# Gated linear attention with a feed-forward layer: longer runs in the first loads, another form of the weight conversion, other places for its steps

## The chip, the cores and the metric

The kernel runs on one core of a Trainium2 chip. The metric is the device time of one execution in microseconds. The engines named here are TensorE (PE, with PEld for its weight loads), VectorE (DVE), ScalarE (ACT), GpSimd (POOL) and SyncE (SP). SP issues every DMA of this kernel, in one queue.

## What is computed

There are 4 batches of 8 heads, 768 tokens and 48 numbers a head, and then a feed-forward layer over all 3,072 tokens. The inputs `q`, `k`, `v` and `alpha` are float32; both weight matrices come as float64.

```python
for t in range(S):
    state = alpha[:, :, t, :, None] * state + np.einsum('bhd,bhe->bhde', k[:, :, t], v[:, :, t])
    y[:, :, t] = np.einsum('bhd,bhde->bhe', q[:, :, t], state)
...
x = np.ascontiguousarray(attn_out.transpose(0, 2, 1, 3)).reshape(B * S, H * D)
...
h = x @ w_in            # 384 to 2048
g = np.maximum(0.01 * h, h)
return (g @ w_out).astype(np.float32)   # 2048 to 384
```

## The kernel before

**Attention.** The work is cut into 24 units: 128 tokens of one batch with all 8 heads. For a unit u, `scans` builds running products of alpha along the tokens (L309) and the products of alpha to the next mark (L315), `scaled_q` and `scaled_k` multiply q and k by them, `scores` multiplies k by q (L351), `mask_scores` copies the scores out on ACT and masks them on POOL, `k_tokens` turns k back, `outputs` adds the masked scores times v to q times the state and splits the result into a high and a low part (L419, L420), and `next_state` updates the state. The units are staggered: scans of unit u+1 are emitted ahead of the scores of unit u.

**Two ways to bring a tile in.** alpha, q and k come with tokens in rows and are needed with the 48 numbers of two heads in rows. For the first nine units (`AHEAD`), `load` (L128) fetches a tile with one token per partition, 8 runs of 48 numbers (192 bytes) each, and `transposed` turns it on PE with four transposes against `ident` (L272) into a PSUM bank. Later units are loaded in runs of four tokens and turned on DVE (L284); this stays. There are two load buffers for each of alpha, q and k (`NL`), so unit u+2 is loaded when unit u has been turned. Each PSUM tile of the attention takes the next of six banks (`bank`, tags "a" and "b" in turn).

**Keeping PE's clock.** `keep_warm` issues fp32 matmuls of `seed` into an idle bank at the start and between the transposes of unit 0. `keep_warm_wide` does so with a tile `zeros` between the transposes of k of unit 0.

**Feed-forward.** Three units (384 tokens) form a block i, eight blocks in all, and the 2,048 inner numbers are cut into 16 slices f. An item is (i, f). `ffn_in` multiplies x by w_in with nine matmuls of 384 columns (high times high, low times high, high times low, over three groups of rows, L487) into one of two banks `ph`, scales on ACT (L490), takes the maximum on DVE (L493), which frees the bank, rounds to the high part on ACT (L495) and takes the low part on DVE (L499). `ffn_out` (L512) multiplies by w_out three items later (`LAG`). Blocks 0 and 1 go first, in turn: (0,0), (1,0), (0,1), (1,1), and so on. Items (0,0) and (1,0) are started beside the last attention units (`STARTS`). Blocks 2 to 7 follow one by one, with the attention of units 9 to 23 woven in between.

**Converting the weights.** [...] Its eight steps before: ACT scales the top words (L238), DVE shifts them (L240) and puts in the sign (L243), ACT rounds to the high part (L246), DVE takes the exponent (L250), subtracts the high part (L252), multiplies the low words by the exponent (L254) and adds both into the low part (L257). `load_weights` fetches slice f into one of four raw buffers with five DMAs. Slices 0 and 1 are converted whole beside units 7 and 8. Slice 2 is converted whole when unit 8 is done, and one step of slice 3 is taken. Later slices are converted in steps between the DVE and ACT instructions of the items of blocks 0 and 1.

**What sets the order.** The framework plans the order on each engine at build time, by its own estimate of durations. Where the code says `tc.issue_after`, or `put(ordered, ...)`, the order is written by hand: every DVE and ACT instruction of items and conversions from (0,1) to the end of block 1 stands in one line per engine. Engines take their instructions in that order; PE, DVE, ACT, POOL and SP meet by semaphores.

Of the kernel before, what the change touches and what calls it, by code (L numbers as in the profile page):

```python
# [9 lines left out]
F32 = mybir.dt.float32  # L10
# [12 lines left out]
def gated_linear_attn_ffn(ctx, tc, q, k, v, alpha, w_in, w_out, out):  # L23
# [29 lines left out]
    NV = 3  # L53
# [5 lines left out]
    LAG = 3  # L59
    SOON, EARLY = 2, 2  # L60
    LEAD = 8
# [11 lines left out]
    def pieces(name, dtype, *shapes):  # L73
# [11 lines left out]

    ident, mask, ones, acc, seed, *rest = pieces(
        "small", F32, (P,), (C,), (1,), (2 * NU,), (NP, C), *[(NP * D,)] * B, *[(DM,)] * NV, *[(NP * PITCH,)] * sum(NL)
    )
# [27 lines left out]
    def load(u, i):  # L116
# [8 lines left out]
        if u < AHEAD:  # L125
            n = H if u or i else H // 2
            for h in range(0, H, n):
                nc.sync.dma_start(  # L128
                    by_token(t)[:, h:h + n, 0:D], src[b, h:h + n, ts, :].rearrange("h t d -> t h d")
                )  # L130
            return
# [21 lines left out]
    nc.vector.memset(ones, 1.0)  # L153
    zeros = cst.tile([P, 4 * C], F32R, name="zeros")
    nc.gpsimd.memset(zeros.bitcast(F32), 0.0)

# [6 lines left out]

    def keep_warm_wide(n):

        for _ in range(2):
            nc.tensor.matmul(idle[:, 0:n], zeros[:, 0:P], zeros[:, 0:n], start=True, stop=True)

    keep_warm(6)
    for i in (0, 1, 2):  # L170
        for t in loads_sb[i]:
            nc.vector.memset(by_token(t)[:, :, D:], 1.0)
    for n in range(max(NL)):
# [3 lines left out]
        load_values(n)  # L177
    make_identity(nc, ident)
    nc.gpsimd.memset(mask, 1.0)
    nc.gpsimd.affine_select(  # L180
# [3 lines left out]
    for i in (0, 1, 2):  # L184
        for t in loads_sb[i]:
            nc.gpsimd.memset(t[:, H * HB:], 1.0)

# [31 lines left out]
    def converting(f, ordered=False):  # L219
# [17 lines left out]
        with nullcontext() if lines["ACT"] else behind("hi", f - 1):  # L237
            put(ordered, "ACT", lambda: nc.scalar.mul(top.bitcast(F32), top.bitcast(F32), 2.0 ** -112))  # L238
        yield
        put(ordered, "DVE", lambda: nc.vector.tensor_scalar(  # L240
            bits, top, 3, 0x7FFFFFF8, ALU.logical_shift_left, ALU.bitwise_and))
        yield
        put(ordered, "DVE", lambda: nc.vector.scalar_tensor_tensor(  # L243
            bits, top, -0x80000000, bits, ALU.bitwise_and, ALU.bitwise_or))
        yield
        made["hi", f] = put(ordered, "ACT", lambda: nc.scalar.copy(hi, val))  # L246
        yield
        pw = cvp.tile([P, 2 * DM], I32, name="pw", bufs=NPW)
        rest = pw.bitcast(F32)
        put(ordered, "DVE", lambda: nc.vector.tensor_scalar(pw, bits, -0x800000, None, ALU.bitwise_and))  # L250
        yield
        put(ordered, "DVE", lambda: nc.vector.tensor_tensor(val, val, hi.bitcast(F32), ALU.subtract))  # L252
        yield
        put(ordered, "DVE", lambda: nc.vector.scalar_tensor_tensor(  # L254
            rest, low.bitcast(U32), 2.0 ** -52, rest, ALU.mult, ALU.mult))
        yield
        made["w", f] = put(ordered, "DVE", lambda: nc.vector.tensor_tensor(lo, rest, val, ALU.add))  # L257

# [7 lines left out]
    def transposed(u, i, name, **kw):  # L266

        src = loaded(u, i)
        if u < AHEAD:
            ps = banks4()  # L270
            for p in range(NP):
                last = nc.tensor.transpose(  # L272
                    ps[:, p, :], by_token(src)[:, 2 * p:2 * p + 2, :].rearrange("t h d -> t (h d)"), ident
                )
                if u == 0 and p % 2:
                    with tc.issue_after(last.ins):
                        if i == 2:
                            keep_warm_wide(4 * C if p == 1 else 2 * C)
                        else:
                            keep_warm(2)  # L280
            return ps
# [196 lines left out]
    def ffn_in(i, f, steps=None):  # L478
# [16 lines left out]
        put(ordered, "ACT", lambda: nc.scalar.copy(gh, t))  # L495
        for step in second:
            next(step, None)
        gl = ffp.tile([P, TB], F32R, name="gl", bufs=LAG + 1)
        made["gl", i, f] = put(ordered, "DVE", lambda: nc.vector.tensor_tensor(gl, t, gh.bitcast(F32), ALU.subtract))  # L499
        return gh, gl  # L500

# [55 lines left out]
    kinds[:] = "a"  # L557

    with behind("x", AHEAD - 1):
        for _ in converting(EARLY, True):  # L560
            pass

    due, emitted, held = 0.0, 0, 0
    new, coming = None, converting(EARLY + 1, True)
    next(coming)
    for n in range(len(items) + LAG):
        slices = 0
        if n < len(items):
# [15 lines left out]
            if n < len(STARTS):  # L584
                pass
            elif i == 0:
                old, new, coming = new or iter(()), coming, converting(f + SOON + 1, True)
                gs[n] = ffn_in(i, f, ((), (coming, new, old, new)))
            elif i == 1:
                gs[n] = ffn_in(i, f, ((new, new), (new,)))  # L590
                next(new, None)
            else:
                gs[n] = ffn_in(i, f)
# [142 lines left out]
```

## Time and profile before

| | |
|---|---|
| Time, median of 3 runs | 538.94 us (538.92 to 539.31) |
| The profiled execution | 538.77 us, its span 537.1 us, granted clock 0.991 |
| PE busy | 518.8 us (97%) in 3,934 instructions |
| DVE busy | 375.0 us (70%) in 703 instructions |
| ACT busy | 234.0 us (44%) in 514 instructions |
| POOL busy | 49.1 us (9%) in 116 instructions |
| DMA | 92,985 packets, 46.67 MB, 57,856 of the packets under 512 bytes |

The span is the time from the first to the last instruction of the profiled execution; the 538.77 us hold what lies around it too. Busy times overlap between engines and say nothing of order. The stages are: units 0 to 8 of the attention and the first conversions up to about 70 us; blocks 0 and 1 of the feed-forward with all other conversions up to about 165 us; blocks 2 to 7 with the other units up to 531 us; and 6 us in which the last results are written.

### The profile page before, as it was taken

The page shows a single profiled execution, that of the slowest core. Times are in us where ns is not written, and L with a number is a line of the kernel's source. Part 1 is how long each engine was busy: PE and PEld are TensorE (multiplying, and loading weights), DVE is VectorE, ACT ScalarE, POOL GpSimd, SP SyncE. Part 2 cuts the span into 40 slices and gives each one's busy share as a digit, 9 for nine tenths or more (in the row PEclk, how much of TensorE's full clock was granted, in tenths as well). Part 3 has the DMA queues.
Part 4 walks back from the last instruction along what each step waited for, and adds up shares of the span by engine and source line. Part 5 has one row for each costly group of instructions (what it writes and reads, how often), then busy time and mean ns, then how long its engine had stood idle before and what let it go on. Part 6 is the DMA issues. An engine that isn't in the chain of part 4 may idle for free.

```text
span 537.1 us, 10383 instructions
## 1 busy us (share of the span) xinstructions
PE 518.8 (97%) x3934; PEld 492.6 (92%) x3934; DVE 375.0 (70%) x703; ACT 234.0 (44%) x514; POOL 49.1 (9%) x116
## 2 busy tenths in 40 slices
PE   8879899999999999999999999999999999999995
PEld 7668789999999899999999999999999999999995
DVE  6778999999988897875675685775777534332331
ACT  2665755555533453435334443344343354233331
POOL 3333510000000011010000001000000000000000
PEclk9999899999999999999999999999999999999998
DMA  9999854454823643533323422523201010001001
GB/s 149 163 179 183 198 140 119 117 131 136 183 53 87 190 117 78 107 81 98 70 67 70 108 69 64 98 50 92 71 0 38 11 35 1 22 1 45 1 1 49
DMA packets 92985, 46.67 MB, mean 87 GB/s; under 512 B 57856, under 2 KB 90112, under 8 KB 92928
## 3 DMA queue, kind: packets, MB, share of 16 engines
q1 hardware_dynamic: 92928, 45.93, 39.0%
q8 instruction: 33, 0.54, 0.4%
q14 instruction: 24, 0.20, 0.1%
HBM read 38.83 MB, written 4.72 MB: 81 GB/s over the span
## 4 chain that ended last, share of the span: by engine, by line
PE 86%; DVE 4%; DMA 3%; issue 2%; ACT 1%; SPq 1%; POOL 1%; ACTq 0%; DVEq 0%; POOLq 0%
PE ph L487 36%; PE b L512 32%; PE a L390 5%; PE a L351 4%; PE a L512 4%; DMA small<-in_alpha_dram 2%; DMA raw<-in_moe_w_in_dram 1%; PE a L374 1%; PE b L272 1%; PE a L411 1%; PE b L390 1%; DVE pc L309 1%; PE b L411 1%; POOL sm L362 1%; DVE rc L315 0%
## 5 line engine op out<-in xcount | busy, mean ns | idle before, releaser
L487 PE MATMUL ph<-large,w 128*128 128x384 f32 x1152 | 227.4, 340 | 2.8 <-DVE t L493 2.8
L487 PEld LDWEIGHTS ph<-large,w 128*128 128x128 f32 x1152 | 201.9, 189 | 5.5 <-DVE t L493 3.9
L512 PE MATMUL b<-w,gh 128*128 128x384 f32 x672 | 170.0, 340 | 0.0
L493 DVE TENSOR_TENSOR t<-ph,t 128x384 f32<-128x384 f32 x128 | 70.5, 551 | 88.7 <-ACT t L490 88.4
L512 PEld LDWEIGHTS b<-w,gh 128*128 128x128 f32 x672 | 119.7, 188 | 2.2 <-issue 0.5
L490 ACT ACTIVATE t<-ph 128x384 f32<-128x384 f32 x128 | 62.6, 489 | 130.1 <-PE ph L487 122.8
L495 ACT CAST gh<-t 128x384 fp32r<-128x384 f32 x128 | 65.7, 514 | 112.8 <-DVE t L493 102.6
L512 PE MATMUL b<-w,gl 128*128 128x384 f32 x336 | 107.4, 336 | 0.0
L499 DVE TENSOR_TENSOR gl<-t,gh 128x384 fp32r<-128x384 f32 x128 | 70.8, 553 | 34.4 <-ACT gh L495 33.2
L512 PEld LDWEIGHTS b<-w,gl 128*128 128x128 f32 x336 | 62.5, 188 | 0.1
L362 POOL TENSOR_SCALAR_AFFINE_SELECT sm<-sm 128x512 f32<-128x512 f32 x33 | 22.8, 705 | 113.3 <-ACT sm L361 113.3
L351 PE MATMUL a<-qs,ks 48*128 48x128 f32 x312 | 30.9, 287 | 0.1
L351 PEld LDWEIGHTS a<-qs,ks 48*128 48x128 f32 x312 | 25.9, 189 | 5.4 <-issue 4.4
L284 DVE STREAM_TRANSPOSE ks<-small 128x512 f32<-128x512 f32 x15 | 16.6, 1121 | 12.3 <-PE a L374 12.3
L390 PE MATMUL a<-sm,small 128*48 128x128 f32 (+1 forms) x312 | 23.2, 282 | 0.1
L319 POOL COPY pe<-pc 128x4 f32<-128x4 f32 x24 | 4.8, 202 | 188.6 <-DVE pc L309 188.6
L309 DVE TENSOR_TENSOR_SCAN pc<-e,small 128x128 f32<-128x128 f32 x60 | 20.1, 398 | 0.5 <-ACT pc L327 0.5
L367 POOL TENSOR_TENSOR small<-us,pe 112x192 f32<-112x192 f32 x20 | 11.9, 594 | 90.2 <-DVE us L432 87.5
L390 PEld LDWEIGHTS a<-sm,small 128*48 128x48 f32 (+1 forms) x312 | 17.1, 132 | 3.2 <-issue 3.0
L361 ACT COPY sm<-a 128x512 f32<-128x512 f32 x24 | 14.0, 585 | 13.8 <-PE b L351 11.1
L512 PE MATMUL a<-w,gh 128*128 128x384 f32 x96 | 20.0, 336 | 0.0
L315 DVE TENSOR_TENSOR_SCAN rc<-e,small 128x511 f32<-128x511 f32 x15 | 19.0, 1270 | 0.2
(86 smaller groups left out, 525.4 us busy)
## 6 DMA issues: line engine op xcount, KB each, us to landing
raw<-in_moe_w_out_dram SPq DMA_DIRECT2D x16, 384.0 KB, 3.9
small<-in_v_dram SPq DMA_DIRECT2D x24, 192.0 KB, 4.0
raw<-in_moe_w_in_dram SPq DMA_DIRECT2D x32, 144.0 KB, 3.9
out_dram<-t SPq DMA_DIRECT2D x24, 192.0 KB, 1.9
small<-in_alpha_dram SPq DMA_DIRECT2D x32, 96.0 KB, 2.3
small<-in_q_dram SPq DMA_DIRECT2D x30, 96.0 KB, 2.2
small<-in_k_dram SPq DMA_DIRECT2D x30, 96.0 KB, 2.2
small<-in_alpha_dram SPq DMA_DIRECT2D x30, 80.0 KB, 2.3
```

Of the source, the lines that this page charges most:

```text
L284: nc.vector.transpose(t.rearrange("r p (j t) -> r p t j", t=T4), src.rearrange("r p (t d) -> r p t d", t=T4)[:, :, :, 0:32],)
L309: nc.vector.tensor_tensor_scan(pc[:, p, :], aT[:, p, :], ones.broadcast_to([P, C]), 1.0, ALU.mult, ALU.mult)
L315: nc.vector.tensor_tensor_scan(flat[2][:, NP * C - 2::-1], flat[0][:, NP * C - 1:0:-1], flat[1][:, NP * C - 2::-1], last, ALU.mult, ALU.add)
L351: nc.tensor.matmul(ss[s][:, p, :], ks[lo:lo + D, p, :], qs[lo:lo + D, p, :], start=True, stop=True)
L362: nc.gpsimd.affine_select(out=sm[s], in_=sm[s], compare_op=ALU.is_ge, fill=0.0, base=0, pattern=[[0, NP], [1, C]], channel_multiplier=-1)
L390: nc.tensor.matmul(y[s][HB * c:HB * c + lhsT.shape[-1], p % 2, :], lhsT, rhs, skip_group_check=True, **kw)
L487: nc.tensor.matmul(ph, w_in_of(f, wn, g), xt[:, g, :], start=n == 0, stop=n == 3 * NG - 1)
L490: put(ordered, "ACT", lambda: nc.scalar.mul(t, ph, 0.01))
L493: put(ordered, "DVE", lambda: nc.vector.tensor_tensor(t, ph, t, ALU.max))
L495: put(ordered, "ACT", lambda: nc.scalar.copy(gh, t))
L499: made["gl", i, f] = put(ordered, "DVE", lambda: nc.vector.tensor_tensor(gl, t, gh.bitcast(F32), ALU.subtract))
L512: nc.tensor.matmul(po[j], gt[:, js], w_out_of(f, wn), start=f == 0 and n == 0, stop=f == NF - 1 and n == 2)
```

## The change

- `load` for the first nine units: partition (j, p) now holds four tokens (4j to 4j+3) of the heads 2p and 2p+1, in two runs of 192 numbers (768 bytes). It is one DMA a tile for unit 0 too, where alpha came in two.
- `transposed` for these units: for each of the four tokens n and each of the two heads s, one ordinary matmul with 64 columns of the tile (48 numbers of the token, then 16 of what follows) as the stationary operand and `turn` as the moving one. `turn` is the identity with its columns reordered; POOL copies it from `ident` once. Each matmul writes 64 partitions and every fourth of 512 columns.
- The memsets at the start follow the new layout; `zeros` and `keep_warm_wide` are gone, and `keep_warm(2)` stands in their place.
- `converting`: the low part no longer comes from the subtraction of the high part. The bits below the high part are cut out of the top word by two shifts in place, added to the scaled low word, and multiplied by the exponent. It is still eight steps, six of them on DVE.
- Places: five of the eight steps of slice 2 stand ahead of the items, the other three in item (0,1). Slice f+1 is finished in item (0,f), and slice f+2 is begun there and carried five steps far by item (1,f). In items with such steps, the low part `gl` (L499) now comes after one step, and the rest of the steps after it.

```diff
-        if u < AHEAD:
-            n = H if u or i else H // 2
-            for h in range(0, H, n):
-                nc.sync.dma_start(
-                    by_token(t)[:, h:h + n, 0:D], src[b, h:h + n, ts, :].rearrange("h t d -> t h d")
-                )
+            nc.sync.dma_start(
+                t[:, 0:2 * PITCH].rearrange("r (s n) -> r s n", s=2)[:, :, 0:RUN],
+                src[b, :, ts, :].rearrange("(p s) (j t) d -> j p s (t d)", s=2, t=T4),
+            )
...
-    zeros = cst.tile([P, 4 * C], F32R, name="zeros")
-    nc.gpsimd.memset(zeros.bitcast(F32), 0.0)
...
+    nc.gpsimd.tensor_copy(turn.rearrange("r (p j) -> r p j", p=NP), ident.rearrange("r (j p) -> r p j", p=NP))
...
         put(ordered, "DVE", lambda: nc.vector.tensor_scalar(
-            bits, top, 3, 0x7FFFFFF8, ALU.logical_shift_left, ALU.bitwise_and))
+            bits, top, 3, 4, ALU.logical_shift_left, ALU.bitwise_or))
...
+        put(ordered, "DVE", lambda: nc.vector.tensor_scalar(
+            top, top, 23, 23, ALU.logical_shift_left, ALU.arith_shift_right))
+        yield
+        pw = cvp.tile([P, 2 * DM], I32, name="pw", bufs=NPW)
+        put(ordered, "DVE", lambda: nc.vector.tensor_scalar(pw, bits, -0x800000, None, ALU.bitwise_and))
+        yield
         made["hi", f] = put(ordered, "ACT", lambda: nc.scalar.copy(hi, val))
         yield
...
-        put(ordered, "DVE", lambda: nc.vector.tensor_tensor(val, val, hi.bitcast(F32), ALU.subtract))
-        yield
-        put(ordered, "DVE", lambda: nc.vector.scalar_tensor_tensor(
-            rest, low.bitcast(U32), 2.0 ** -52, rest, ALU.mult, ALU.mult))
-        yield
-        made["w", f] = put(ordered, "DVE", lambda: nc.vector.tensor_tensor(lo, rest, val, ALU.add))
+        rest = top.bitcast(F32)
+        put(ordered, "DVE", lambda: nc.vector.scalar_tensor_tensor(
+            rest, low.bitcast(U32), 2.0 ** -32, top, ALU.mult, ALU.add))
+        yield
+        made["w", f] = put(ordered, "DVE", lambda: nc.vector.scalar_tensor_tensor(
+            lo, rest, 2.0 ** -20, pw.bitcast(F32), ALU.mult, ALU.mult))
...
         if u < AHEAD:
-            ps = banks4()
-            for p in range(NP):
-                last = nc.tensor.transpose(
-                    ps[:, p, :], by_token(src)[:, 2 * p:2 * p + 2, :].rearrange("t h d -> t (h d)"), ident
-                )
-                if u == 0 and p % 2:
+            ps = bank()
+            for n in range(T4):
+                for s in (0, 1):
+                    at = s * PITCH + n * D
+                    last = nc.tensor.matmul(
+                        ps[HB * s:HB * (s + 1), n::T4], src[:, at:at + HB], turn, start=True, stop=True, skip_group_check=True
+                    )
+                if u == 0 and n % 2:
                     with tc.issue_after(last.ins):
...
-        for step in second:
+        for step in second[:1]:
             next(step, None)
         gl = ffp.tile([P, TB], F32R, name="gl", bufs=LAG + 1)
         made["gl", i, f] = put(ordered, "DVE", lambda: nc.vector.tensor_tensor(gl, t, gh.bitcast(F32), ALU.subtract))
+        for step in second[1:]:
+            next(step, None)
...
+    new, coming = converting(EARLY, True), converting(EARLY + 1, True)
     with behind("x", AHEAD - 1):
-        for _ in converting(EARLY, True):
-            pass
+        for _ in range(5):
+            next(new)
...
             elif i == 0:
-                old, new, coming = new or iter(()), coming, converting(f + SOON + 1, True)
-                gs[n] = ffn_in(i, f, ((), (coming, new, old, new)))
+                gs[n] = ffn_in(i, f, ((new,), (new, new, coming)))
             elif i == 1:
-                gs[n] = ffn_in(i, f, ((new, new), (new,)))
-                next(new, None)
+                gs[n] = ffn_in(i, f, ((), (coming, coming, coming, coming)))
+                new, coming = coming, converting(f + EARLY + 1, True)
```

More of the change, by code (lines that the diff above doesn't have):

```diff
@@ L59, in gated_linear_attn_ffn @@
     LAG = 3
-    SOON, EARLY = 2, 2
+    EARLY = 2
     LEAD = 8
@@ L84, in pieces @@
         return parts
-    ident, mask, ones, acc, seed, *rest = pieces(
-        "small", F32, (P,), (C,), (1,), (2 * NU,), (NP, C), *[(NP * D,)] * B, *[(DM,)] * NV, *[(NP * PITCH,)] * sum(NL)
+    ident, turn, mask, ones, acc, seed, *rest = pieces(
+        "small", F32, (P,), (P,), (C,), (1,), (2 * NU,), (NP, C), *[(NP * D,)] * B, *[(DM,)] * NV, *[(NP * PITCH,)] * sum(NL)
     )
@@ L162, in keep_warm, with tails @@
             nc.tensor.matmul(idle[:, 0:C], seed[:, 0, :], seed[:, 1, :], start=True, stop=True)
-    def keep_warm_wide(n):
-        for _ in range(2):
-            nc.tensor.matmul(idle[:, 0:n], zeros[:, 0:P], zeros[:, 0:n], start=True, stop=True)
     keep_warm(6)
+    def tails(t):
+        return t[:, 0:2 * PITCH].rearrange("r (s n) -> r s n", s=2)[:, :, RUN:]
     for i in (0, 1, 2):
         for t in loads_sb[i]:
-            nc.vector.memset(by_token(t)[:, :, D:], 1.0)
+            nc.vector.memset(tails(t), 1.0)
     for n in range(max(NL)):
@@ L185, in gated_linear_attn_ffn @@
         for t in loads_sb[i]:
-            nc.gpsimd.memset(t[:, H * HB:], 1.0)
+            nc.gpsimd.memset(t[:, 2 * PITCH:], 1.0)
     runs = [(0, D, 0, 1, D), (D, GAP, NG * D, NG, 1), (HB, D, NP * D, 1, D), (BR, GAP, (NP + NG) * D, NG, 1)]
@@ L245, in converting @@
         yield
+        put(ordered, "DVE", lambda: nc.vector.tensor_scalar(
[4 more added lines that the diff above has]
+        yield
         made["hi", f] = put(ordered, "ACT", lambda: nc.scalar.copy(hi, val))
         yield
-        pw = cvp.tile([P, 2 * DM], I32, name="pw", bufs=NPW)
-        rest = pw.bitcast(F32)
-        put(ordered, "DVE", lambda: nc.vector.tensor_scalar(pw, bits, -0x800000, None, ALU.bitwise_and))
+        rest = top.bitcast(F32)
+        put(ordered, "DVE", lambda: nc.vector.scalar_tensor_tensor(
+            rest, low.bitcast(U32), 2.0 ** -32, top, ALU.mult, ALU.add))
         yield
-        put(ordered, "DVE", lambda: nc.vector.tensor_tensor(val, val, hi.bitcast(F32), ALU.subtract))
-        yield
-        put(ordered, "DVE", lambda: nc.vector.scalar_tensor_tensor(
-            rest, low.bitcast(U32), 2.0 ** -52, rest, ALU.mult, ALU.mult))
-        yield
-        made["w", f] = put(ordered, "DVE", lambda: nc.vector.tensor_tensor(lo, rest, val, ALU.add))
+        made["w", f] = put(ordered, "DVE", lambda: nc.vector.scalar_tensor_tensor(
+            lo, rest, 2.0 ** -20, pw.bitcast(F32), ALU.mult, ALU.mult))
     def convert(f):
@@ L269, in transposed @@
         if u < AHEAD:
-            ps = banks4()
-            for p in range(NP):
-                last = nc.tensor.transpose(
-                    ps[:, p, :], by_token(src)[:, 2 * p:2 * p + 2, :].rearrange("t h d -> t (h d)"), ident
-                )
-                if u == 0 and p % 2:
-                    with tc.issue_after(last.ins):
[L277 to L281, printed above, removed]
+            ps = bank()
[6 more added lines that the diff above has]
+                if u == 0 and n % 2:
+                    with tc.issue_after(last.ins):
+                        keep_warm(2)
+            return ps.rearrange("r (p t) -> r p t", p=NP)
         t = atp.tile([P, NP, C], F32, name=name, **kw)
@@ L557, in gated_linear_attn_ffn @@
     kinds[:] = "a"
+    new, coming = converting(EARLY, True), converting(EARLY + 1, True)
     with behind("x", AHEAD - 1):
-        for _ in converting(EARLY, True):
-            pass
+        for _ in range(5):
+            next(new)
     due, emitted, held = 0.0, 0, 0
-    new, coming = None, converting(EARLY + 1, True)
-    next(coming)
     for n in range(len(items) + LAG):
```

## The prediction

> **What bounds the kernel now.** I read the busy time by stage first, cut where the chain of waits changes character. The columns are the stretch in us, its length, then busy us and instruction count of PE, PEld, DVE, ACT and POOL, and last the granted TensorE clock, the DMA share and GB/s.
>
> ```profile
> 5.69:32.05 26.36, 22.06 (x267) 17.95 (x266) 22.21 (x52) 14.09 (x37) 8.10 (x21) 1.00 1.21 172
> 32.05:52.78 20.73, 18.43 (x261) 15.56 (x260) 16.76 (x37) 11.44 (x30) 6.56 (x15) 0.92 1.03 177
> 52.78:76.41 23.63, 21.14 (x211) 18.32 (x206) 22.50 (x41) 14.24 (x31) 8.23 (x9) 0.93 0.75 172
> 76.41:172.40 95.99, 95.99 (x552) 95.97 (x552) 92.63 (x151) 49.27 (x88) 0.65 (x2) 1.00 0.47 118
> 172.40:179.00 6.60, 4.77 (x27) 4.14 (x25) 6.49 (x14) 1.86 (x4) 0.38 (x2) 1.00 0.76 209
> 179.00:531.00 352.00, 352.00 (x2616) 336.50 (x2616) 213.06 (x405) 140.60 (x321) 21.80 (x52) 1.00 0.24 58
> ```
>
> From 76.41 us to 172.4 and from 179 to 531 PE has no idle time at full clock. The feed-forward matmuls set the end there, and the change touches none of them. DVE is also nearly full up to 172 (92.63 of 95.99), but there it only keeps pace: taking conversion work off it between 76 and 172 buys nothing, because PE has no gap to close. The change can move the end only by moving the moment at which that solid block begins, 76.41. Before it no engine is full all the time, so I looked at the steps there one by one.
>
> Units 1 to 4 of the attention repeat a pattern. In the timeline of PE the columns are start, duration, what, and in brackets the idle time before it with its releaser.
>
> ```profile
> 19.48 0.65 PE L390 MATMUL b<-sm,small 128*64 128x128 f32 x8 [0.82 <-POOL sm L362]
> 20.06 0.66 PE L272 MATMUL b<-small 128*128 128x128 f32 x4
> ...
> 23.22 0.60 PE L272 MATMUL b<-small 128*128 128x128 f32 x4
> 23.66 0.60 PE L272 MATMUL a<-small 128*128 128x128 f32 x4
> 25.09 0.65 PE L390 MATMUL b<-sm,small 128*64 128x128 f32 x8 [0.83 <-POOL sm L362]
> ```
>
> A period is 25.09 - 19.48 = 5.61 us. Three groups of four transposes lie in it (alpha behind the masked products, then q and k), at a pitch of 0.44 each (23.66 - 23.22), and PE idles 0.83 waiting for GpSimd's mask. So PE has room for 0.83 us a period, and the alpha group stands in the loop that sets the period.
>
> **Transposes become matmuls (L272).** Four transposes a tile give way to eight fp32 matmuls with 64 stationary columns. The rows above show an ordinary fp32 matmul as two instructions (x8 for the four products that line 403 puts into one bank) and a transpose as one (x4 a tile), so 4 instructions a tile become 16. Two narrow matmuls into different halves of the output partitions overlap. The weight loads show it:
>
> ```profile
> 45.07 0.42 PEld L272 LDWEIGHTS b<-small 128*128 128x128 f32 x4 [0.17 <-issue]
> 45.66 0.41 PEld L390 LDWEIGHTS b<-sm,small 128*64 128x64 f32 x8 [0.17 <-issue]
> ```
>
> Eight instructions of the paired narrow form take 0.41, as long as four transposes. Sixteen take 0.82 to 0.88, so a tile costs +0.44 and a unit +1.32. Bounds: no gain is possible, as the array streams twice as many columns; unpaired it would be 16 x 0.11 = 1.76, +1.32 a tile. I take +0.44, since L390 has the same shape. The strided output (every fourth column) has no row here; I take it as free, with the unpaired price as the other end.
>
> The page "TensorE: Matmul & The Clock Gate" of the Trainium skill (section Terms) gives the transpose mode as four times faster for fp32. By that an overlapped pair would take 4 x 0.11, a tile four such pairs, 1.76 against 0.44. The trace speaks against it: a matmul of two 0.11 us instructions is twice a transpose. It stays as a rival below.
>
> **First units' loads (L128).** 1,024 runs of 192 bytes a load become 256 runs of 768. Two places show the old loads late:
>
> ```profile
> 14.45 0.66 PE L272 MATMUL b<-small 128*128 128x128 f32 x4 [1.24 <-DMA small<-in_alpha_dram]
> ```
> ```profile
> 26.73 3.17 SPq L128 DMA_DIRECT2D small<-in_alpha_dram x1
> ```
> ```profile
> 33.21 2.68 DMA raw<-in_moe_w_in_dram
> ```
> ```profile
> 36.00 0.88 ACT L238 ACTIVATE raw<-raw 128x768 f32<-128x768 f32 x1 [2.58 <-DMA raw<-in_moe_w_in_dram]
> ```
> ```profile
> 37.14 0.66 PE L272 MATMUL b<-small 128*128 128x128 f32 x4 [1.99 <-ACT us L430]
> ```
>
> Unit 2's alpha is 1.24 late on PE. Later one load holds SP's queue for 3.17 us; behind it stands the first weights' load, whose last piece (from 33.21) arrives 2.58 after ACT wanted it, and ACT's queue, then PE, stand still. With a quarter of the runs I expect neither wait. What is late next is PE: counted with its longer groups, unit 2's transposes end at about 15.0, where they end now, so the first wait pays for the longer groups of units 0 to 2 and for a start about 0.3 later (the first alpha no longer comes in halves, and one more GpSimd copy makes `turn`). I set L309 of unit 2 at -0.1. The groups of the alphas of units 3, 4 and 5 then stand in the 5.61 loop: +0.44 x 3 = +1.3; q and k, +0.88, nearly fill the 0.83 of idle.
>
> ```profile
> 32.05 1.37 DVE L309 TENSOR_TENSOR_SCAN pc<-b,small 128x128 f32<-128x128 f32 x4 [0.87 <-PE b L272]
> ...
> 39.15 1.36 DVE L309 TENSOR_TENSOR_SCAN pc<-b,small 128x128 f32<-128x128 f32 x4 [0.62 <-ACT pc L327]
> ...
> 52.78 1.35 DVE L309 TENSOR_TENSOR_SCAN pc<-b,small 128x128 f32<-128x128 f32 x4
> ```
>
> These are the scans of units 5, 6 and 8. From 5 to 6 took 7.10 with the late weights; without them it is a PE period of 5.61 - 0.83 + 1.32 = 6.1, less about 0.2 for overlap: -1.2. From 6 to 8 took 13.63, 6.8 a unit, part of it at half clock:
>
> ```profile
> 40.00:42.00 2.00, 2.00 (x26) 1.91 (x25) 1.82 (x5) 0.74 (x2) 0.37 (x2) 0.50 1.33 141
> ...
> 60.00:62.00 2.00, 2.00 (x7) 2.00 (x7) 2.00 (x5) 0.47 (x2) 0.00 (x0) 0.50 1.01 243
> ```
> ```profile
> 59.98 3.20 PE L487 MATMUL ph<-large,w 128*128 128x384 f32 x9
> ```
>
> The clock fell to 0.50 after PE's 1.99 us stop ahead of 37.14, and again near 59. With the first stop gone, the longer groups (+1.32 a unit) come at full clock and make, by my choice, as much as the slow clock cost, about 6.75 a unit: -0.1. Sum at unit 8's scan: -0.1 + 1.3 - 1.2 - 0.1 = -0.1. So the first half of the change is a trade, PE time for waits.
>
> **From 52.78 to 76.41** DVE is busy 22.50 of 23.63 and binds, with three conversions in its queue.
>
> ```profile
> 97.04 0.55 DVE L250 TENSOR_SCALAR pw<-bits 128x768 int32<-128x768 int32 x1
> 97.50 0.55 DVE L493 TENSOR_TENSOR t<-ph,t 128x384 f32<-128x384 f32 x1
> 97.97 0.95 DVE L252 TENSOR_TENSOR bits<-bits,w 128x768 f32<-128x768 f32 x1
> 98.84 0.55 DVE L499 TENSOR_TENSOR gl<-t,gh 128x384 fp32r<-128x384 f32 x1
> ```
>
> By start times a one-tensor operation on 128x768 occupies DVE 0.46 (97.50 - 97.04), a two-tensor one 0.87 (98.84 - 97.97). The new form drops the subtraction L252 (0.87) and adds a shift pair with one tensor (0.46): -0.4 a conversion. The shift writes every second word, which no row shows; at the slow price it takes 0.87 and saves 0. I take 0.46, that of L240, which reads every second word. Conversions 0 and 1 lie in this stretch: -0.8. The other operations change operands, not kind.
>
> ```profile
> 63.80 0.56 DVE L493 TENSOR_TENSOR t<-ph,t 128x384 f32<-128x384 f32 x1 [0.37 <-ACT t L490]
> ...
> 69.35 0.56 DVE L499 TENSOR_TENSOR gl<-t,gh 128x384 fp32r<-128x384 f32 x1 [0.58 <-ACT gh L495]
> ```
>
> These two waits, 0.95, come from PE being late: item (0,0) took 3.20 at half clock; the same nine take 1.83 at full clock in the row at 76.41 below. PE's idle hole ahead of it takes the longer groups of unit 8 (+0.88). If that spell goes, PE is 1.4 earlier and the 0.95 goes: -0.95.
>
> ```profile
> 71.22 0.95 DVE L243 SCALAR_TENSOR_TENSOR bits<-raw,bits 128x768 int32<-128x768 int32 x1
> ...
> 74.93 0.96 DVE L257 TENSOR_TENSOR w<-pw,bits 128x768 fp32r<-128x768 f32 x1
> ```
> ```profile
> 76.41 1.83 PE L487 MATMUL ph<-large,w 128*128 128x384 f32 x9 [0.95 <-DVE t L493]
> ```
>
> Conversion 2 now runs whole ahead of item (0,1)'s L493, and item (0,2) waits for that L493 to free its bank. After the change five of eight steps stand in front. From 71.22: 0.87 + 0.46 + 0.46, then L493 0.47, two-tensor 0.87, L499 0.47, last step 0.96: 75.78. Before, the low weights were ready at 75.89 (74.93 + 0.96), and the L493 came only then. Item (0,2) now waits for the weights alone and starts at about 75.85: -0.55. No new wait blocks others: the steps after L499 stand behind it, and what follows on DVE is the next item's L493, 18 matmuls of PE work away, 3.13 us at the 0.174 each of the stretch from 76.41 (95.99 / 552).
>
> From 76.41 on each f has 0.4 less DVE work under a full PE: 0. Raw weight buffers come free one step later, but there are four of them, and a weight is asked for two f and more ahead of its use: 0. The dropped `zeros` memset and wide matmuls lie in the first 10 us, in the 0.3 above.
>
> **Sum:** -0.1 - 0.8 - 0.95 - 0.55 = -2.4 us against the profiled execution's own 538.77 (span 537.1): **536.4**. The median of the runs, 538.94, lies 0.17 above that execution, which is inside what I can resolve. About 0.2%, 1.1 us, is what a measurement of this kernel can tell from no change.
>
> **Rivals.**
> *The half-clock spell stays* (or the shift saves nothing). The longer groups leave PE short of activity somewhere, and item (0,0) again takes 3.2. Then -0.95 and part of the rest go: about -0.9, 537.9, between 537.3 and 539. For: PE still waits for DVE's scan ahead of item (0,0). Against: the groups fill that hole. The page named above says (Part 4: PE-mode transpose) that transposes don't count as PE activity for the clock. No run here shows it; by it the new matmuls would hold the clock better, which would favour the forecast by some points.
> *PE becomes the bound (slower).* Every alpha group lengthens its loop: 9 x 0.44 = 4.0. Between 32.05 and 52.78 PE idled 20.73 - 18.43 = 2.30, and 1.99 of it was the stop for the weights, so the three periods there have 0.1 each to hide q and k: 0.78 each, 2.3. The waits give back 2.2, the conversions 1.2: +2.9, 541.7. It decides as soon as PE's idle time per unit is under the 1.32 added and the clock stays as it was; 0.83 is near enough that the order of the work on PE settles it. The unpaired price would take it further.
> *Loads far ahead let the plan run earlier:* the 0.83 wait vanishes too, as alpha is transposed ahead of the masked products: three to four units give 0.44 more back, 534.9.
> *The fourfold price:* +1.32 a tile, 27 tiles, 36 us, less the 9.1 that PE idles in the first three rows above: about 565. The instruction counts speak against it.
>
> **Chances.** Forecast 0.45 (its own range 535.4 to 537.6), half clock 0.22, PE bound 0.20, earlier plan 0.10, fourfold 0.03. Faster by over 0.2%: 0.43 + 0.07 + 0.10 = 0.60; within: 0.02 + 0.14 + 0.04 = 0.20; slower 0.20. The range 535.0 to 541.7 leaves out the fourfold price (0.03), the upper half of PE bound (0.10) and half of the earlier plan (0.05).
>
> **What would show it.** Right: no DMA wait ahead of L238 and of unit 2's alpha, tile groups of some 0.88, clock 1.00 between 38 and 63, item (0,0) in 1.6, item (0,2) near 74, and the time from item (0,2) to the end unchanged at 460.7 (537.1 - 76.41). Wrong: groups of 1.7, a clock of 0.50 over item (0,0), unit 8's scan after 54, or new gaps on PE after 76.

## The result, and the profile after

The changed kernel takes 542.8 us in the median of 20 runs (539.65 to 544.44), the kernel before 539.13 on the same chip (20 runs): a ratio of 1.0058, with a 95% interval of 1.0041 to 1.0074. It is 3.1 us slower (0.0058 of 539), where 2.4 us faster was forecast. The profiled execution took 544.34 us, its span 542.5, so it stands near the upper end of the runs; what follows compares it with the profiled execution before (span 537.1), and takes the size of each effect from the ratios. One execution of a kernel told below (alpha by token, halves) took 1,303.3 us and is left out of its ratio.

The running product of alpha on DVE opens every unit. Its timeline in the changed kernel (start, duration, what, idle time before it and its releaser):

```profile
9.27 1.37 DVE L306 TENSOR_TENSOR_SCAN pc<-a,small 128x128 f32<-128x128 f32 x4 [7.54 <-PE a L272]
...
16.73 1.36 DVE L306 TENSOR_TENSOR_SCAN pc<-b,small 128x128 f32<-128x128 f32 x4 [0.93 <-PE b L272]
...
22.56 1.37 DVE L306 TENSOR_TENSOR_SCAN pc<-b,small 128x128 f32<-128x128 f32 x4
...
40.60 1.36 DVE L306 TENSOR_TENSOR_SCAN pc<-b,small 128x128 f32<-128x128 f32 x4
46.99 1.36 DVE L306 TENSOR_TENSOR_SCAN pc<-b,small 128x128 f32<-128x128 f32 x4
...
61.34 1.36 DVE L306 TENSOR_TENSOR_SCAN pc<-b,small 128x128 f32<-128x128 f32 x4
```

These are units 0, 1, 2, 5, 6 and 8. The table sets the stretches between them beside those before and those of three experiments told below.

| Stretch, us | before | changed | conversion alone | long runs, old transposes | halves, no warming |
|---|---|---|---|---|---|
| scan of unit 0 starts at | 5.69 | 9.27 | 6.21 | 5.51 | 6.05 |
| unit 0 to 1 | 4.17 | 7.46 | 4.17 | 4.17 | 4.17 |
| 1 to 2 | 5.35 | 5.83 | 5.08 | 4.23 | 6.10 |
| 2 to 5 | 16.84 | 18.04 | 16.84 | 16.87 | 18.51 |
| 5 to 6 | 7.10 | 6.39 | 8.35 | 5.87 | 6.39 |
| 6 to 8 | 13.63 | 14.35 | 13.65 | 12.54 | 14.35 |
| unit 8's scan to item (0,2) | 23.63 | 19.74 | 20.52 | 23.66 | 19.68 |
| item (0,2) starts at | 76.41 | 81.08 | 74.82 | 72.85 | 75.25 |
| item (0,2) to the end of the span | 460.7 | 461.4 | 460.3 | 461.5 | 460.5 |

The last row says that the end is set by the moment at which item (0,2) starts, as before. That moment comes 4.67 later. Of this 6.87 is lost by unit 1's scan (16.73 against 9.86) and 1.69 from there to unit 8's (61.34 against 52.78 is 8.56), and 3.89 is won back behind it. Where the start loses it, the chain of waits shows (start, length, what):

```profile
0.82 0.44 SPq L146
1.26 0.06 issue
1.32 0.57 SPq L146
1.89 0.04 issue
1.94 3.82 DMA small<-in_alpha_dram
5.76 0.14 issue
5.89 1.12 PE a L272 x8
7.01 1.15 PE ph L159 x4
8.16 1.05 PE a L272 x8
9.22 1.15 PE ph L159 x4
10.37 1.87 PE b L272 x16
12.24 0.87 PE a L272 x14
13.12 1.53 PE ph L159 x12
14.65 0.36 PE a L272 x2
15.01 0.64 PE ph L159 x4
15.65 1.02 PE b L272 x16
```

Three things stand in it. **First the order of SP's queue:** two loads of v (L146) are issued before the first alpha. They were behind the loads of alpha, q and k before. A load in long runs spans two runs and the pad between them, and DVE's memsets write the pads (L167, at 1.44); the reading here is that alpha has to follow them, so that v, which follows nothing, goes ahead. Loads that span no pad go first again, as an experiment below shows. The loads before spanned pads too, with memsets from 1.46 on, and were issued at 0.82 all the same; why the framework takes the two shapes differently is not shown. Alpha is issued at 1.94 instead of 0.82 and lands at 5.76. **Second PE's speed:** PE stood idle for 1.43 us ahead of 5.89, and until 12.24 eight instructions, half a tile, take 1.05 to 1.12 and a tile's sixteen 1.87, where the last row shows 1.02 for sixteen. **Third the warming matmuls of unit 0 (L159)** are pieces of the chain: 1.15 twice between alpha's matmuls, then 12 instructions, 1.53, ahead of the last pair of k's tile, for which DVE waits.

From there on PE is full. The busy time by stage (length, then busy us and count of PE, PEld, DVE, ACT, POOL, granted clock, DMA share, GB/s), in the cuts used before:

```profile
5.69:32.05 26.36, 26.16 (x346) 23.19 (x348) 17.57 (x40) 10.03 (x26) 6.04 (x16) 1.00 0.53 140
32.05:52.78 20.73, 20.73 (x373) 18.65 (x371) 15.87 (x37) 12.70 (x34) 6.18 (x15) 1.00 0.79 196
52.78:76.41 23.63, 22.25 (x321) 18.84 (x318) 22.06 (x43) 14.92 (x36) 6.79 (x13) 1.00 0.65 159
```

PE was busy 22.06 and 18.43 us in the first two rows before, and is busy 26.16 and 20.73 now; the DMA share fell from 1.21 and 1.03 to 0.53 and 0.79. The wait for unit 2's alpha is gone, and up to 52.78 so is PE's idle time. The wait for the first weights is 0.58 instead of 2.58, and PE no longer stops for it:

```profile
38.71 0.94 ACT L234 ACTIVATE raw<-raw 128x768 f32<-128x768 f32 x1 [0.58 <-DMA raw<-in_moe_w_in_dram]
```

The groups of the turning matmuls have the length that was worked out (columns of the grouped lines: busy us, mean ns of one, idle before):

```profile
L272 PE MATMUL b<-small 128*64 128x128 f32 x272 | 20.8, 284 | 1.0 <-PE a L272 1.0
L272 PE MATMUL a<-small 128*64 128x128 f32 x160 | 13.0, 292 | 1.4 <-DMA small<-in_alpha_dram 1.4
```

33.8 us in 432 instructions are 1.25 for a tile of 16 with the slow start in it; before they were 17.3 in 108 (10.8 and 6.5), 0.64 for a tile of four. The difference, 0.6, holds the slow start. At full speed a tile's sixteen take 1.02 in the chain above; in the kernel "halves, no warming", told below, tiles start 0.87 apart (5.81, 6.68, 7.55), against 0.44.

### The profile page after: what moved, and what is told of

It reads as the page before. It is cut to its first block, busy times and chain, and to the rows that moved or that the text cites. A ratio compares the mean times of both kernels' runs of the same rounds, so it can differ in the third digit from the quotient of the medians.

```text
span 542.5 us, 11006 instructions
## 1 busy us (share of the span) xinstructions
PE 529.5 (98%) x4262; PEld 504.3 (93%) x4262; DVE 371.1 (68%) x703; ACT 235.9 (43%) x514; POOL 47.9 (9%) x116
## 4 chain that ended last, share of the span: by engine, by line
PE 90%; DVE 5%; DMA 1%; issue 1%; ACT 0%; SPq 0%; ACTq 0%; DVEq 0%
PE ph L484 35%; PE b L511 32%; PE a L387 5%; PE a L348 5%; PE a L511 4%; PE b L272 2%; PE a L272 2%; PE a L371 1%; PE a L408 1%; DVE pc L306 1%; PE ph L159 1%; PE b L387 1%; DMA small<-in_alpha_dram 1%; DVE t L490 1%; DVE w L254 0%
## 5 line engine op out<-in xcount | busy, mean ns | idle before, releaser
L484 PE MATMUL ph<-large,w 128*128 128x384 f32 x1152 | 224.0, 338 | 2.1 <-DVE t L490 1.8
L359 POOL TENSOR_SCALAR_AFFINE_SELECT sm<-sm 128x512 f32<-128x512 f32 x33 | 21.2, 653 | 107.8 <-ACT sm L358 107.8
L281 DVE STREAM_TRANSPOSE ks<-small 128x512 f32<-128x512 f32 x15 | 16.7, 1123 | 13.3 <-PE a L371 13.3
L387 PE MATMUL a<-sm,small 128*64 128x128 f32 (+1 forms) x312 | 23.2, 278 | 0.0
L272 PE MATMUL b<-small 128*64 128x128 f32 x272 | 20.8, 284 | 1.0 <-PE a L272 1.0
L387 PEld LDWEIGHTS a<-sm,small 128*64 128x64 f32 (+1 forms) x312 | 17.1, 129 | 3.1 <-issue 2.9
```

The costliest lines, as they stand in the source:

```text
L272: last = nc.tensor.matmul(ps[HB * s:HB * (s + 1), n::T4], src[:, at:at + HB], turn, start=True, stop=True, skip_group_check=True)
L281: nc.vector.transpose(t.rearrange("r p (j t) -> r p t j", t=T4), src.rearrange("r p (t d) -> r p t d", t=T4)[:, :, :, 0:32],)
L359: nc.gpsimd.affine_select(out=sm[s], in_=sm[s], compare_op=ALU.is_ge, fill=0.0, base=0, pattern=[[0, NP], [1, C]], channel_multiplier=-1)
L387: nc.tensor.matmul(y[s][HB * c:HB * c + lhsT.shape[-1], p % 2, :], lhsT, rhs, skip_group_check=True, **kw)
L484: nc.tensor.matmul(ph, w_in_of(f, wn, g), xt[:, g, :], start=n == 0, stop=n == 3 * NG - 1)
```

## The experiments

Each effect in us is (ratio - 1) times 539; its interval reaches 0.8 to 1.5 us to each side. The kernel before ran beside each kernel on the same chip, with medians of 538.8 to 540.1, so the ratios compare and the medians do not quite.

| Kernel | Median, us | Ratio to before [95%] | us |
|---|---|---|---|
| changed | 542.80 | 1.0058 [1.0041, 1.0074] | +3.1 |
| conversion alone | 536.94 | 0.9958 [0.9942, 0.9974] | -2.3 |
| loads and matmuls alone | 543.89 | 1.0082 [1.0059, 1.0105] | +4.4 |
| first loads in halves | 540.62 | 1.0017 [1.0002, 1.0031] | +0.9 |
| no warming between | 539.51 | 0.9996 [0.9979, 1.0012] | -0.2 |
| halves, no warming | 537.93 | 0.9977 [0.9960, 0.9994] | -1.2 |
| formula alone, old places | 543.29 | 1.0073 [1.0047, 1.0100] | +3.9 |
| transposes twice | 542.67 | 1.0062 [1.0040, 1.0085] | +3.3 |
| long runs, old transposes | 537.14 | 0.9959 [0.9942, 0.9977] | -2.2 |
| longer warming in front | 541.62 | 1.0034 [1.0016, 1.0052] | +1.8 |
| alpha by token | 538.51 | 0.9974 [0.9960, 0.9989] | -1.4 |
| alpha by token, halves | 538.41 | 0.9967 [0.9944, 0.9990] | -1.8 |
| the same, no warming | 536.07 | 0.9947 [0.9927, 0.9967] | -2.9 |

**The two halves of the change.** The kernel before with the new form of `converting` and the new places, and the changed kernel with those of before:

```diff
-        put(ordered, "DVE", lambda: nc.vector.tensor_tensor(val, val, hi.bitcast(F32), ALU.subtract))
+        put(ordered, "DVE", lambda: nc.vector.tensor_scalar(
+            top, top, 23, 23, ALU.logical_shift_left, ALU.arith_shift_right))
...
-                gs[n] = ffn_in(i, f, ((), (coming, new, old, new)))
+                gs[n] = ffn_in(i, f, ((new,), (new, new, coming)))
```

> The conversion's new form and places alone, loads and transposes as before. Theory A (the loss lies in the start of units 0 and 1): this part keeps the gain the prediction gave it, 1.4 to 2.5 us under the kernel before, ratio 0.995 to 0.9975, first scan near 5.7 us as before. Theory B (the conversion's new order is what costs): not below the kernel before, ratio 1.000 or more, and item (0,2) later than 76.4 us.

> Loads and turning matmuls as changed, conversion and its places as before. Theory A: all of the loss and none of the conversion's gain: ratio 1.008 to 1.012, second scan near 16.7 us. Theory B: the loss is gone, ratio 1.000 or less.

The conversion alone gives 2.3, all of it behind unit 8's scan (20.52 against 23.63, while the scan itself comes 1.52 later). Its ratio lies where theory A put it. The loads and matmuls alone cost 4.4. The sum, +2.1, is the change within the intervals, so the loss lies wholly in the loads and the matmuls. But unit 1's scan starts at 13.54 there, not near 16.7 as expected: PE runs at full speed from its first tile on in that execution. The conversion alone also tells something about the half-clock spell. ACT still waits for the weights in it, and the clock falls in that stage:

```profile
36.17 0.89 ACT L238 ACTIVATE raw<-raw 128x768 f32<-128x768 f32 x1 [2.50 <-DMA raw<-in_moe_w_in_dram]
```
```profile
32.05:52.78 20.73, 18.61 (x236) 15.30 (x234) 15.29 (x36) 11.69 (x31) 5.77 (x15) 0.84 1.09 178
52.78:76.41 23.63, 22.16 (x240) 19.89 (x240) 22.94 (x42) 15.02 (x33) 8.49 (x10) 1.00 0.71 162
```
```profile
61.27 1.83 PE L489 MATMUL ph<-large,w 128*128 128x384 f32 x9
```

Yet item (0,0) takes 1.83 at a clock of 1.00. The weights' wait and the transposes are as before here, and the spell over item (0,0) is gone all the same.

**The start.** Units 0 and 1 load each head of a pair by a DMA of its own, with a memset for each half, so that no load crosses a pad; then the warming matmuls between unit 0's matmuls are taken out; then both:

```diff
+            if u < 2:
+                for s in (0, 1):
+                    nc.sync.dma_start(
+                        t[:, s * PITCH:s * PITCH + RUN], src[b, s::2, ts, :].rearrange("p (j t) d -> j p (t d)", t=T4)
+                    )
+                return
...
-                if u == 0 and n % 2:
-                    with tc.issue_after(last.ins):
-                        keep_warm(2)
```

> The changed kernel, but the tiles of units 0 and 1 come in two DMAs of one head each and the tails are set by two memsets, so that no load waits for a memset and alpha goes ahead of v. Theory A: the first scan begins 2 to 3 us earlier than 9.27, the second 3 us or more earlier than 16.73, and the end moves with them: ratio 0.998 to 1.001 to the kernel before. Rival (PE's longer groups bind units 1 to 8 whatever the start): the end moves by under 1 us, ratio 1.004 to 1.007.

> The changed kernel without the clock-keeping matmuls between the turning matmuls of unit 0; the loads stay late. Theory A with these matmuls in the way: first scan at about 8, second at about 13.5, ratio 1.000 to 1.003. Rival (they bring the clock up): PE stays at half clock longer, the second scan not before 16, ratio 1.006 or more.

> The changed kernel with both cures of the start together: units 0 and 1 in halves without a wait for the memsets, and no clock-keeping matmuls between the turning matmuls. Theory A (the start is the whole loss): second scan near 11, ratio 0.992 to 0.996, below the conversion alone (0.9958), as the weights' wait is gone too. Rival B (the turning matmuls also cost 1 us or more over units 2 to 8): second scan near 11 all the same, but the time from the second to the ninth scan stays at 44.5 us or more, against 42.9 before, and the ratio lies at 0.996 to 0.999, not below the conversion alone.

The halves bring 2.2 (+0.9 instead of +3.1), the warming matmuls 3.3 (-0.2), both together 4.4 (-1.2): they overlap, as both stand in the chain quoted above. Unit 1's scan starts at 12.14 with the halves and at 12.11 without the warming, both as theory A said. With both cures, that chain begins so:

```profile
0.81 0.18 issue
0.99 0.48 DVE small L157
...
1.54 2.92 PE ph L165 x12
4.46 1.56 PE a L279 x16
6.03 0.02 issue
6.05 1.37 DVE pc L310 x4
```

Alpha is no piece of it any more: it has landed when the six warming matmuls end, PE has no hole, and the first scan starts at 6.05, the second at 10.22 (16.73 in the changed kernel). So the start costs the changed kernel about 4.4 us, more than its whole loss. Rival B holds as well: from the second to the ninth scan this kernel takes 45.35, over the 44.5 that was named, and its ratio isn't below that of the conversion alone.

**Half speed at the start.** The changed kernel with more warming matmuls in front, so that PE has no hole before alpha:

```diff
-    keep_warm(6)
+    keep_warm(14)
```

> Edit: the changed kernel with 14 instead of 6 warming matmuls ahead of the first tile, so that PE doesn't stand still for 1.43 us before alpha arrives at 5.76. Theory 'slow start by idling': PE reaches full speed because it has been busy without a hole; the turning matmuls of unit 0 and the warming ones between them then take 0.64 for four instead of 1.15, unit 0's scan starts near 8.3 (9.27 now), unit 1's near 14 (16.73), and the time falls by 2 to 3 us, to about 540, the lower of the two groups of its times. Rival 'the order of the queues': v first and the wait for the memsets hold alpha until 5.76, and the longer warming stands in front of it besides; the start is 9.3 or later and the time stays at 542 to 544.

```profile
1.53 5.32 PE L159 MATMUL ph<-small 128*128 128x128 f32 x28 [1.53 <-DVE small L167]
6.79 0.66 PE L272 MATMUL a<-small 128*64 128x128 f32 x8
7.37 0.71 PE L159 MATMUL ph<-small 128*128 128x128 f32 x4
...
9.24 1.09 PE L272 MATMUL b<-small 128*64 128x128 f32 x16
```

This is PE's timeline. The same eight instructions take 0.66 instead of 1.12, sixteen 1.09 instead of 1.94, though the first of them starts 0.9 later. Unit 0's scan starts at 8.72, unit 1's at 14.46, 2.3 earlier. By the ratios the time falls by 1.3 us, but the two intervals overlap. The theory holds for the start; its 2 to 3 us was too much, and v still goes ahead of alpha here. In the changed kernel, the profile's column of the granted clock doesn't show the half speed:

```profile
5.89:12.24 6.35, 6.35 (x44) 5.24 (x46) 2.87 (x7) 0.00 (x0) 0.38 (x2) 1.00 0.61 164
```

It says 1.00 over a stretch in which 44 instructions run, where the kernel with more warming runs 79. The Trainium skill, "TensorE: Matmul & The Clock Gate", section "Part 1: The HAM clock gate", says that PE begins at half clock and gets the full one only after about 3.4 us of sustained work, in windows that run freely. The traces agree as far as they go: PE works without a hole from 1.53 here, and is at full speed at 6.79; in the changed kernel, with the hole of 1.43, only at 12.24, after 6.35 us of work without a hole. They don't measure the 3.4 us, and a hole alone does not decide: in loads and matmuls alone PE stood idle for 1.05 us ahead of 5.51, and the same eight instructions took 0.66 at once.

**The price of the matmuls and the gain of the runs, each by itself.** The kernel before with every transpose of units 1 to 8 issued twice (+0.44 us of PE a tile), and the kernel before with its loads in long runs (those of units 0 and 1 in halves, as above), where the transposes read these tiles as they read the old ones:

```diff
-            for p in range(NP):
+            for p in [*range(NP)] * (2 if u else 1):
                 last = nc.tensor.transpose(
```

> The kernel before, with the four transposes of each tile of units 1 to 8 issued twice into the same bank: the 0.44 us of PE a tile that the turning matmuls add, and nothing else of the change. Theory A: PE's idle time hides most of it, ratio 1.000 to 1.003. Rival B (PE's price is on the path): units 2 to 8 take 2 us or more longer, ratio 1.004 to 1.008.

> The kernel before with the long runs in the loads of the first nine units and the four transposes a tile as they were. The transposes then turn numbers of other tokens into the rows, so what units 0 to 8 compute is not the reference's; the work is the same. It shows what the long runs bring if their price on PE is left away. Theory A (as predicted, 2.2 us of waits for loads and weights): ratio 0.994 to 0.997, no wait of 2 us ahead of the first weights' scaling. Rival: the transfers were hidden behind PE and DVE anyway, ratio 0.998 to 1.001.

Rival B holds for the transposes, theory A for the runs. The transposes issued twice cost 3.3 us: 10.6 us of PE time (24 tiles at 0.44), a third of which reaches the end. At unit 8's scan it is more than half: the scan starts at 58.59, 5.81 late. From there to item (0,2) the stretch is 2.57 shorter than before (21.06 against 23.63), and DVE, which binds there, has 19.79 us of work in it instead of 22.50:

```profile
58.59:79.65 21.06, 18.11 (x184) 15.95 (x182) 19.79 (x37) 11.27 (x26) 7.17 (x9) 1.00 0.56 135
```

While PE holds the scan back, DVE does three steps of conversion 0 ahead of it (L250, L252, L254) that stood behind it before. So part of what PE's extra work costs at that scan is won back behind it. The long runs give 2.2. Their column in the table of stretches shows where: 1.12 from unit 1 to 2, 1.23 from 5 to 6, 1.09 from 6 to 8. The weights' wait there is

```profile
31.28 0.92 ACT L244 ACTIVATE raw<-raw 128x768 f32<-128x768 f32 x1 [0.46 <-DMA raw<-in_moe_w_in_dram]
```

instead of 2.58. The three effects, -2.3, -2.2 and +3.3, make -1.2, which is what the kernel with a mended start measures; with the start's 4.4 they make +3.2, against +3.1 for the change. That they meet within 0.1 is luck: each is known to about 1 us, and the conversion and the doubled transposes partly win the same time behind unit 8's scan (3.11 and 2.57 by themselves, 3.95 in the kernel with the mended start). The column "halves, no warming" less the column "long runs, old transposes" is the matmuls' price by stretch: +1.87, +1.64, +0.52, +1.81 from unit 1 to unit 8, the last with the new conversion's steps in it.

**Only alpha back to the old way.** Alpha of the first nine units by token, with transposes; q and k in long runs with turning matmuls; then the halves for q and k; then no warming in unit 0:

```diff
+        if u < AHEAD and i == 0:
+            n = H if u else H // 2
+            for h in range(0, H, n):
+                nc.sync.dma_start(
+                    by_token(t)[:, h:h + n, 0:D], src[b, h:h + n, ts, :].rearrange("h t d -> t h d")
+                )
+            return
```

> Edit: the changed kernel with alpha of the first nine units as before (one token a partition, 192-byte runs, two DMAs for unit 0, four transposes a tile); q and k keep long runs and turning matmuls. Theory 'price on the path by tile': the alpha groups stand in the loop of the units, q and k fill PE's idle 0.83. The periods of units 2 to 5 fall from 5.84 to about 5.6, unit 0's scan starts near 6, and unit 8's scan near 53.5 (61.34 changed, 52.78 before); with the conversions' 2.3 and part of the weights' wait (two thirds of the runs are shorter in number) the time is 535 to 537.5. Rival 'all turning matmuls are on the path': 18 tiles instead of 27 at 0.44 still cost about 2.3 of the 3.4, the second to ninth scan takes over 44.5 us (42.92 before, 45.35 with three tiles), and the time is 537 to 539.

> Edit: as the kernel with alpha by tokens, and q and k of units 0 and 1 come in two DMAs of one head each, with a memset for each half, so that no load waits for another part's memset. Theory 'price on the path by tile': a start as before the change (unit 0's scan 5.7 to 6.1, unit 1's 9.9 to 10.4) and the same periods as the kernel with alpha by tokens: 534.7 to 537. Rival 'all turning matmuls are on the path': the start is as before, but the second to ninth scan takes over 44.5 us, and the time is 536.5 to 538.5, no better than the conversion alone.

> Edit: as the kernel with alpha by tokens and q and k of units 0 and 1 in halves, without the warming matmuls between the tiles of unit 0. Theory 'start and price add up': the first two scans start near 5.8 and 10.0, the second to ninth scan takes 44.6 as with those matmuls, so unit 8's scan starts near 54.6 (56.74 with them, 54.30 with the conversion alone), and the time is 536 to 537, some 2 us under the same kernel with them and equal to the conversion alone. Rival 'the warming matmuls are needed': PE runs longer at half speed without them, unit 8's scan starts at 56 or later and the time stays at 538 to 539.

The second to the ninth scan take 45.13 and 44.64 us in the first two (44.61 in the changed kernel, 45.35 with its start mended, 42.92 before): over the 44.5 that was named, the second by little, so the rival holds. q and k don't hide in PE's 0.83 of idle time. Nor did the periods of units 2 to 5 fall to 5.6: the three take 18.81 to 19.29 in these kernels, against 18.04 in the changed one and 16.84 before. How much of what remains is their matmuls and how much alpha's short runs, which are back, these kernels don't separate. Without the warming matmuls the scans of units 0 and 1 start at 5.31 and 9.49, that of unit 8 at 54.38 as worked out (54.6), and the time is 536.07, 0.9947 of before: the fastest of all, though its interval overlaps that of the conversion alone (0.9958). Both beat both kernels.

**The formula without the new places.** The kernel before with the new steps of `converting`, called from the old places (of the diff of the first experiment, only the part above the line of dots):

> Loads as before, the conversion's new form with the old places of its steps. If the form (0.4 us of DVE a conversion, no wait for the rounding) makes the gain: ratio 0.996 to 0.998. If the places make it: 0.999 to 1.001, and item (0,2) still waits for L493.

It was slower by 3.9 us, outside both ranges. Item (0,2) starts at 74.31, 2.1 earlier than before, but then each f takes longer. PE's timeline:

```profile
84.26 1.83 PE L489 MATMUL ph<-large,w 128*128 128x384 f32 x9
...
90.86 1.83 PE L489 MATMUL ph<-large,w 128*128 128x384 f32 x9
...
97.47 1.83 PE L489 MATMUL ph<-large,w 128*128 128x384 f32 x9
```

and DVE's, the wait that stands in each f:

```profile
84.84 0.56 DVE L501 TENSOR_TENSOR gl<-t,gh 128x384 fp32r<-128x384 f32 x1 [0.64 <-ACT gh L497]
...
91.44 0.56 DVE L501 TENSOR_TENSOR gl<-t,gh 128x384 fp32r<-128x384 f32 x1 [0.63 <-ACT gh L497]
```

An f is 6.61 (97.47 - 90.86) where 36 matmuls need 6.26 (36 times 0.174). The rounding on ACT is the sixth step in the new form and was the fourth. Called from the old places, it falls where DVE's subtraction stood, between the maximum and `gl`; DVE has nothing to do there and waits 0.64 for ACT. The new places are a condition of the new form, not an addition to it.

## Why the prediction was wrong, and where it was right

**The step that failed** is "a start about 0.3 later", within the term for unit 2's scan: -0.1 was given, +7.35 measured (22.56 against 15.21) in this execution. The working looked at what the start's instructions last. It did not ask which loads could still be issued first: in the new shape two loads of v went ahead of the first alpha, and with loads that span no pad they did not. Nor did it count the warming matmuls as work in PE's line, 1.15 a pair at half speed, or what a hole of 1.43 does to that speed. With the start mended in both ways unit 2's scan starts at 16.32, 1.1 late: the rest of the term was mis-sized by that much, since the groups of unit 1 and 2 (+1.87 in 1 to 2) cost more than the wait for alpha (1.12) gave. The price on PE is the second step that failed: with the start mended unit 8's scan is still 2.79 late (55.57 against 52.78), where -0.1 was worked out. So the time would have been 1.2 better than before, half of the 2.4 that was forecast.

**The other terms in order.** *Alpha groups of units 3 to 5:* +1.3 forecast, +1.20 measured (18.04 - 16.84), but +1.67 with the start mended, and 1.97 to 2.45 with alpha turned by transposes again: the number was near, and that alpha alone makes it while q and k hide is not borne out. *The weights' wait:* -1.2 forecast, -0.71 measured; the wait is down to 0.58, and the period between is 6.39, where 6.1 less 0.2 was worked out. *Units 6 to 8:* -0.1 forecast, +0.72 measured. There the longer groups did run at full clock, but they cost 1.81, and the slow clock had cost 1.09 (with long runs alone, at a clock of 1.00, these units take 12.54). *Behind unit 8's scan:* -2.3 forecast in three parts, -3.89 measured here and -3.11 with the conversion alone. What was cut out of DVE was sized well, with the shift at its fast price (0.56 for 128x768, in place and with every second word written):

```profile
68.75 0.56 DVE L242 TENSOR_SCALAR raw<-raw 128x768 int32<-128x768 int32 x1
69.22 0.56 DVE L246 TENSOR_SCALAR pw<-bits 128x768 int32<-128x768 int32 x1
69.69 0.95 DVE L251 SCALAR_TENSOR_TENSOR raw<-raw 128x768 f32<-128x768 uint32 x1
...
74.81 0.56 DVE L490 TENSOR_TENSOR t<-ph,t 128x384 f32<-128x384 f32 x1 [0.62 <-ACT t L487]
75.95 0.56 DVE L496 TENSOR_TENSOR gl<-t,gh 128x384 fp32r<-128x384 f32 x1 [0.58 <-ACT gh L492]
```

The shift is L242. But the two waits of DVE did not go, as the last two rows of the changed kernel show: 1.20 against 0.95. That term failed, and the stretch got shorter than was forecast in part for a reason that the forecast did not have: when unit 8's scan came, DVE had one step of conversion 0 left, where four were left before.

```profile
61.34:81.08 19.74, 18.36 (x203) 16.16 (x203) 18.34 (x35) 11.57 (x28) 5.76 (x9) 1.00 0.50 124
```

That leaves it 18.34 us of work in the stretch, where it had 22.50. The spell at half clock did go as forecast (item (0,0) took 1.82). Of the two causes named, longer groups and the first stop gone, the first suffices (1.83 with the transposes issued twice) and the second does not (3.03 with long runs alone, where ACT's wait is 0.46); the new conversion suffices too, which the forecast hadn't seen, and why is not shown. *From item (0,2) on:* 0 forecast, +0.7 here, -0.7 to +1.4 over the kernels but the one with the old places.

**The rivals.** "PE becomes the bound" named 541.7 and the right side. Its mechanism is shown up to unit 8's scan: PE is full from 6 to 53 us, q and k are paid for, and the price there, 5.81 with the transposes issued twice and 5.84 by the stretches above, is near the 6.3 (4.0 + 2.3) it was given. But some 2.6 of it comes back behind that scan, so that 3.3 reaches the end, and without the slow start the change would be 1.2 faster: this rival alone would not have made it slower. Its time came out near by luck, because another cost, which neither case had, took the place of the missing half. The fourfold price is refuted by a tile's 0.87 to 1.02. As to the rival of the half clock, transposes hold the clock here too: with them issued twice, and nothing else changed, the granted clock is 1.00 from 32.05 to 63 us, where it fell to 0.50 before. Of the signs, the clock of 1.00 between 38 and 63 came, and item (0,0) ran at full clock (the 1.6 named for it is less than the 1.83 of the prediction's own row); unit 8's scan at 61.34, after the 54 that was to show the forecast wrong, came too.

**Still open:** 5 of the 20 runs of the changed kernel lie at 539.65 to 540.85 and 15 at 542.13 to 544.44. A start at full speed in some executions would fit, but loads and matmuls alone ran with one in its profiled execution (unit 1's scan at 13.54) and its runs show no lower group. It wasn't settled.

## What to carry to other kernels

When a load's shape changes, ask first what else writes the columns it now spans, and what can pass it in its queue: here the first loads in their new shape, over pads that six memsets of 0.29 us in all fill, were issued behind loads of v; loads that span no pad gave 2.2 us back, more than the rest of the change gained. Warming matmuls between real ones are work in PE's line, and worth their place only where PE would else be idle; warming that ends as the first data arrive does the same and delays nothing (4.46 in "halves, no warming"), while warming past that moment put the first tile off by 0.9. An engine's idle time per period isn't room for new work unless that work can stand in the hole: of 10.6 us put beside 0.83 of idle a unit, more than half reached unit 8's scan and a third the end.

## What the runs showed of the hardware

PE ran at about half its speed after a hole of 1.43 us early in the execution for 6.35 us, while the granted clock was given as 1.00; it is seen only in the lengths (0.66 or 1.12 for the same eight instructions) and counts (44 or 79 in the same 6.35 us). After a hole of 1.05 us, in loads and matmuls alone, it was not seen. One step of a conversion took 1.67 instead of 0.95 once in the changed kernel, and PE waited 0.30 for it. The last step of the same conversion took 1.38 in the kernel before and 1.97 with the conversion alone, with GpSimd at work beside it each time; whether that is the reason no run here shows:

```profile
71.62 1.67 DVE L254 SCALAR_TENSOR_TENSOR w<-raw,pw 128x768 fp32r<-128x768 f32 x1
73.22 0.98 DVE L496 TENSOR_TENSOR gl<-t,gh 128x384 fp32r<-128x384 f32 x1
```

Writing every fourth column of a PSUM bank into different halves of its partitions cost nothing that shows: eight instructions took 0.66, eight of the same shape with dense output (L390 before) 0.65.
